# A kernel of attention, soft experts and a two-layer net: its rarely taken branch is put behind all products of the first expert layer

## The chip, the cores and the metric

The kernel runs on one core of one Trainium2 chip. The time is that of one execution on the device, in microseconds (us). Three runs of the kernel before the change gave 556.49, 556.83 and 557.16, median 556.83.

The engines: TensorE (PE, with its weight loads as PEld), VectorE (DVE), ScalarE (ACT), GpSimd (POOL) and SyncE (SP), which issues nearly all DMA transfers here. They run side by side and wait for one another by semaphores, which are counters.

## The reference

Three stages in a row, in float32:

```
attn:   scores = q k^T / 8 + bias(head, distance); keys kept: the first n_global
        and the last n_local up to the query; softmax; times v
        (4 batches, 8 heads, 768 positions, 64 wide; n_global = 8, n_local = 96)
x       = attn as 3072 tokens x 512
experts: logits = x @ phi                        # 32 slots, 4 for each of 8 experts
        d = softmax of logits over the tokens;  slot_in = d^T @ x
        slot_out[e] = relu(slot_in[e] @ w1[e]) @ w2[e]     # 512 x 1024, 1024 x 512
        c = softmax of logits over the slots;  x = c @ slot_out
net:    h = x @ w_in (512 x 2048);  g = relu(h)^2;  out = g @ w_out (2048 x 512)
```

## The kernel before, in words

The kernel runs in three stretches. Up to about 200 us it computes the attention in 48 units and routes each finished chunk of tokens to the slots; from about 254 us on it runs the two-layer net in five parts of unequal width (`WIDTHS`), each over 12 blocks of 256 tokens. The change lies between them, in the expert stage.

**Order.** The schedule is written out by hand: each engine runs its instructions in the order of the code. SyncE issues loads in that order too, and a load whose target is still being read holds back all loads behind it.

**Weights and places.** The expert weights w1_0 to w1_7 and w2_0 to w2_7 (2 MB each) and the raw 64-bit words of the net's first part (`win_0`, `wout_0`, 1 MB each) come in the order of `items`. `SLOTS` gives each a place: p0 to p7 hold w1; s0 to s2 hold w2_0 to w2_2; then p0, p1, p4, p5 take w2_3 to w2_6, p2 win_0, p7 w2_7 and p3 wout_0. A place is free when the products with what it held are done. `more()` issues the next load; w2_7 goes in four parts. `load_part(1)` brings the words of the second part into p0 and p1.

**The expert stage on TensorE.** `w1_of(e)` (L605 to L610) multiplies the slots' inputs by w1_e, 16 instructions in the trace, into two banks `pre0`, `pre1`. `hidden` (L671) evicts these (DVE and ACT), multiplies by a selecting matrix `si` (L678), runs seven warm-up products that compute nothing (`warm`), and takes the relu into `hZ` (L680). `w2_of(e)` (L684 to L690) multiplies by w2_e, 16 instructions in the trace, into `pSO`. Then come the sum's transposes and the first product of the net.

**Combine weights.** `combine` (L590) computes the softmax over the slots for all tokens. `copies(k)` (L649, DVE) repeats the result of six token tiles four times; `spread(k)` (L653) transposes them on TensorE (L658), ACT writes them into `cst` (L660) and DVE subtracts the rounded part (L661). There are four such groups, k = 0 to 3; they stand behind `w2_of(2)` to `w2_of(5)`.

**The branch.** The masks of the attention hold only for small n_local and n_global. A flag decides at L628 whether `general`, a slow path for any values (the dense path), computes everything again. With these inputs it is not taken. Five of the eight `w1_of` and `combine` stand ahead of it. The dense path uses the places of w2_3 and w2_4 for its own data, multiplies by w1 again (loading each into w2_3's place), and loads w2_3 and w2_4 again at its end (L636, L637): 344 loads in all. The compiled program has a short piece of its own for the side that skips it: each engine raises its counter by what the dense path would have raised it, so that what follows waits for the same values on both sides. SyncE does this for the eight counters to which loads report in turn; each of these instructions first waits until all loads issued on its counter have landed.

The lines around the branch:

```
    for e in range(EARLY):
        w1_of(e, wt[f"w1_{e}"])
        if SLOTS[nxt] == f"p{e}":
            more()
    combine()
    with tc.If(cond != 0, label="dense"):
        ...
    for e in range(EARLY, E):
        w1_of(e, wt[f"w1_{e}"])
        while nxt < NI and SLOTS[nxt] in [f"p{i}" for i in range(e + 1)]:
            more()
```

Of the kernel before, what the change touches and what calls it, by code (L numbers as in the profile page):

```python
# [7 lines left out]
F32 = mybir.dt.float32  # L8
F32R = mybir.dt.float32r
# [8 lines left out]
DM, NS, E, F = 512, 32, 8, 1024  # L18
DFF = 2048
NT = B * S  # L20
P = 128
# [7 lines left out]
NPRE = 8  # L29
# [10 lines left out]
def attention_moe_ffn(ctx: ExitStack, tc, qk, vx, nl, ng, phi, w1, w2, w_in, w_out, consts, relw, out):  # L40
    nc = tc.nc
    V, G = nc.vector, nc.gpsimd
# [5 lines left out]
    def full(name, shape, dt=F32):  # L48
        return cp.tile(shape, dt, tag=name, name=name)

    con = full("con", [P, C_R2])
# [16 lines left out]
    post = tc.alloc_tile_pool(name="post", bufs=1, side="right")  # L68
# [7 lines left out]
    def warm(n, src, dst):  # L76
        z = src.bitcast(BF16)
        for _ in range(n):
            nc.tensor.matmul(dst[:, 0:TB], lhsT=z[:, 0:P], rhs=z[:, 0:TB], start=True, stop=True)

    idle = aps.tile([P, 512], F32, tag="m", name="idle", bufs=4)
# [95 lines left out]
    def words(src, q):  # L177
        f0 = starts[q]
        return src[f0 * DM : (f0 + WIDTHS[q]) * DM].bitcast(I32).rearrange("(p c) -> p c", p=P)
# [3 lines left out]
    first = [(f"{n}_0", words(w, 0), [P, 2 * 4 * WIDTHS[0]], I32) for n, w in (("win", w_in), ("wout", w_out))]  # L183
    items[-1:-1] = first[:1]
    items += first[1:]
    NI = len(items)
    wt = {}
    SLOTS = [f"p{i}" for i in range(NPRE)] + ["s0", "s1", "s2"] + [f"p{i}" for i in (0, 1, 4, 5, 2, 7, 3)]

    def slot(tag, shape, dt, name):  # L190
        return (pre if tag[0] == "p" else stream).tile(shape, dt, tag=tag, name=name)

    def load_w(i, part=0, parts=1):
        name, src, shape, dt = items[i]
        if part == 0:
            wt[name] = slot(SLOTS[i], shape, dt, name)
        n = shape[1] // parts
        ps = slice(part * n, part * n + n)
        nc.sync.dma_start(wt[name][:, ps], src[:, ps])
# [302 lines left out]
    for i in range(NU - 2):  # L502
# [35 lines left out]
        if 4 <= i < 4 + NPRE * PARTS:  # L538
            load_w((i - 4) // PARTS, (i - 4) % PARTS, PARTS)
# [10 lines left out]
    i = NU - 2  # L550
# [26 lines left out]
    nxt = NPRE  # L577
    for _ in range(3):
        load_w(nxt)
        nxt += 1  # L580
# [9 lines left out]
    def combine():  # L590
        n = NT // P
        wide = rm.unsqueeze(2).broadcast_to([P, n, NS])
        V.tensor_reduce(rm, c_tok, axis=AX.X, op=ALU.max)
        V.tensor_tensor(c_tok, c_tok, wide, op=ALU.subtract)
        nc.scalar.activation(c_tok, c_tok, AF.Exp)
        V.tensor_reduce(rm, c_tok, axis=AX.X, op=ALU.add)
        V.tensor_scalar(rm, rm, EPS, None, op0=ALU.add)
        V.reciprocal(rm, rm)
        V.tensor_tensor(c_tok, c_tok, wide, op=ALU.mult)
# [5 lines left out]
    def w1_of(e, a):  # L605
        for n in range(2):
            for kc in range(4):
                z = e * 4 * NS + kc * NS
                nc.tensor.matmul(pp[n][kc * NS : kc * NS + NS, :], lhsT=slotZ[:, z : z + NS], rhs=a[:, kc, n * 512 : n * 512 + 512],  # L609
                                 start=e == 0, stop=e == E - 1)  # L610

    def more():
        nonlocal nxt
        if nxt < NI:
            n = 4 if nxt == NI - 2 else 1
            for j in range(n):
                load_w(nxt, j, n)
            nxt += 1

    EARLY = 5  # L620
    for e in range(EARLY):
        w1_of(e, wt[f"w1_{e}"])
        if SLOTS[nxt] == f"p{e}":
            more()
    combine()


    with tc.If(cond != 0, label="dense"):  # L628
        ta, tb = wt["w2_3"], wt["w2_4"]
        general(tc, nc, banks, qk, vx, relw, con, n_f, ta, tb, post, chunk_x, chunk_sums, route_start, route, slope8, ident)  # L630
        a = ta.rearrange("p a c -> p (a c)").rearrange("p (a c) -> p a c", c=F)
        for e in range(EARLY):
            nc.sync.dma_start(a, w1[e])
            w1_of(e, a)
        combine()
        nc.sync.dma_start(ta, w2[3])  # L636
        nc.sync.dma_start(tb, w2[4])  # L637
# [3 lines left out]
    ex = ctx.enter_context(tc.tile_pool(name="ex", bufs=1, side="right"))  # L641
# [3 lines left out]
    crs = {}  # L645

    SP = 6

    def copies(k):  # L649
        cr = crs[k] = ex.tile([P, SP, 4, NS], F32, tag="e", name=f"cr{k}", bufs=2)  # L650
        V.tensor_copy(cr, c_tok[:, SP * k : SP * k + SP, :].unsqueeze(2).broadcast_to([P, SP, 4, NS]))

    def spread(k):  # L653
        cr = crs.pop(k)
        for h in range(2):
            pc = bps.tile([P, 512], F32, tag="post", name=f"pc{k}_{h}", bufs=2)
            for t in range(3):
                nc.tensor.transpose(pc[:, t * P : t * P + P], cr[:, 3 * h + t, :, :].rearrange("p a s -> p (a s)"), ident)  # L658
            tok = slice((SP * k + 3 * h) * P, (SP * k + 3 * h + 3) * P)
            nc.scalar.copy(cst[:, tok], pc[:, 0 : 3 * P])  # L660
            V.tensor_tensor(cst[2 * NS : P, tok], pc[2 * NS : P, 0 : 3 * P], cst[2 * NS : P, tok].bitcast(F32), op=ALU.subtract)  # L661
        if k + 2 < NT // (SP * P):
            copies(k + 2)

    bps = tc.alloc_tile_pool(name="bps", bufs=1, space=PSUM)
    pSO = bps.tile([P, 512], F32, tag="so", name="pSO")


    HS = 8 * NS + 4

    def hidden(hZ):  # L671
        ev = ex.tile([P, F], F32, tag="e", name="ev", bufs=2)
        V.tensor_copy(ev[:, 0:512], pp[0])
        nc.scalar.copy(ev[:, 512:F], pp[1])
        ph = bps.tile([P, 512], F32, tag="sel", name="sel")
        idle = bps.tile([P, 512], F32, tag="post", name="idle3", bufs=2)
        for fc in range(8):
            nc.tensor.matmul(ph[:, NS * fc : NS * fc + NS], lhsT=ev[:, fc * P : fc * P + P], rhs=si, start=True, stop=True)  # L678
        warm(7, con, idle)
        V.tensor_scalar(  # L680
            hZ[:, 0 : E * HS].rearrange("p (e r) -> p e r", r=HS)[:, :, 0 : 8 * NS].rearrange("p e (f s) -> p e f s", s=NS)[:, :, :, 0:4],
            ph[:, 0 : 8 * NS].rearrange("p (f e s) -> p e f s", e=E, s=4), 0.0, None, op0=ALU.max)

    def w2_of(e):  # L684
        c = wt[f"w2_{e}"]
        for fc in range(8):
            g = fc % 4
            z = e * 8 * NS + fc * NS
            nc.tensor.matmul(pSO[g * NS : g * NS + NS, :], lhsT=hZ[:, z : z + NS], rhs=c[:, fc, :],  # L689
                             start=e == 0 and fc < 4, stop=e == E - 1 and fc >= 4)  # L690
# [19 lines left out]
    def load_part(q):  # L710
        raw[q] = []
        for nm, src, tag in (("win", w_in, "p0"), ("wout", w_out, "p1")):
            t = slot(tag, [P, 8 * WIDTHS[q]], I32, f"{nm}_{q}")
            nc.sync.dma_start(t, words(src, q))
            raw[q].append(t)

    def conv_in(q):
        W = WIDTHS[q]
        if q:
            f = slot("p4", [P, 4, W], F32, f"winf{q}").rearrange("p a c -> p (a c)")  # L720
        else:
            f = hZ[:, E * HS : E * HS + 4 * W]
        wq[q] = {"f": f.rearrange("p (a c) -> p a c", c=W)}
        for c0 in range(0, 4 * W, 512):
            yield from convert(raw[q][0], c0, f[:, c0 : c0 + 512], f"i{q}")
            yield
# [95 lines left out]
                V.tensor_tensor(o[:, cs], pa[:, cs], o[:, cs], op=ALU.add)  # L822
                eng.dma_start(out[k * P : k * P + P, cs], o[:, cs])

    for e in range(EARLY, E):
        w1_of(e, wt[f"w1_{e}"])
        while nxt < NI and SLOTS[nxt] in [f"p{i}" for i in range(e + 1)]:
            more()
        if e == E - 2:
            hZ = slot("p6", [P, 4096], F32, "hZ")  # L830
            G.memset(hZ[:, 0 : E * HS], 0.0)
    hidden(hZ)
    copies(0)
    copies(1)
    raw[0] = [wt["win_0"], wt["wout_0"]]
    w2_of(0)
    cu = slot("s0", [P, 4096], F32R, "cu")
    cst = cu[:, 0:NT]
    for e in range(1, E):
        if e == E - 1:  # L840
            load_part(1)
        w2_of(e)
        if 2 <= e < 6:
            spread(e - 2)
        if e == 5:
            for _ in conv_in(0):
                pass
# [3 lines left out]
    idle = bps.tile([P, 512], F32, tag="post", name="idle4", bufs=2)  # L851
# [9 lines left out]
    idle = fps.tile([P, 512], F32, tag="acc", name="idle5", bufs=3)  # L861
# [9 lines left out]
    next(c1)  # L871
    next(c0)
    warm(13, con, idle)
    oacc = [slot(t, [P, 8, DM], F32, f"oacc{i}") for i, t in enumerate(("p3", "p5", "p7"))]
    steps = [(q, n) for q in range(len(WIDTHS)) for n in range(NBLK)]
    AHEAD = 2
    for k in range(AHEAD):
# [16 lines left out]
    for i, (q, n) in enumerate(steps):  # L894
# [3 lines left out]
        for m in range(TB // P):  # L898
            j = 2 * n + m
# [169 lines left out]
```

## Time and profile before

| | us |
|---|---|
| median of three runs | 556.83 |
| profiled execution | 557.27 |
| its span, first to last instruction | 555.3 |
| PE busy | 532.4 (96%) |
| DVE busy | 399.3 (72%) |
| ACT busy | 310.7 (56%) |
| POOL busy | 165.5 (30%) |
| DMA, mean over the span | 161 GB/s |

The profile is of one execution. A row of a view names the engine, the line of the kernel (L689), the operation and the tiles, as out<-in with buffer numbers left out: all tiles of expert weights are `w`. "xN" is a count, and brackets hold the idle time before a row and what ended it. A "q" behind an engine (SPq) means its instruction queue, which waits, branches and issues transfers. The ends of TensorE's products are modelled; the start of the next one is the better mark. The granted clock is a share of TensorE's full 2.4 GHz; 0.50 is 1.2 GHz.

### The profile page before, as it was taken

To read this page: it belongs to the slowest core of one execution; us is meant where nothing else is said; L and a number is where in the kernel's file an instruction comes from. 1 tells how busy PE (TensorE), PEld (TensorE's weight loads), DVE (VectorE), ACT (ScalarE), POOL (GpSimd) and SP (SyncE) were. 2 spreads that over 40 slices of the span, in tenths; PEclk is the share of its full clock that TensorE was granted. 3 is DMA by queue.
4 is the path that set the end of the run, shared out by engine and by line. 5 is a ranking of instruction groups with operands and counts; after the bars stand their busy time and mean duration, and the time that the engine had idled before them with its cause. 6 is when DMAs were issued, how large, how long until landed. Compare 5 with 4: busy or idle time off the path is not lost.

```text
span 555.3 us, 10260 instructions
## 1 busy us (share of the span) xinstructions
PE 532.4 (96%) x3676; PEld 396.3 (71%) x3676; DVE 399.3 (72%) x998; ACT 310.7 (56%) x815; POOL 165.5 (30%) x147
## 2 busy tenths in 40 slices
PE   7999999999999999997999999999999999999997
PEld 4776767676767743345778687878888878888885
DVE  4888878888888771369778798796956857645553
ACT  3877778887877610236666556555544444534441
POOL 0000000000000001004375457543764536544441
PEclk9999999999999989999999999999999999999999
DMA  7789999998863589790440404011030000002333
GB/s 254 216 289 307 323 294 312 309 335 298 291 191 88 206 305 416 281 408 2 151 152 0 152 1 152 0 62 52 2 113 2 1 1 0 1 1 100 125 117 113
DMA packets 25834, 89.22 MB, mean 161 GB/s; under 512 B 3120, under 2 KB 3760, under 8 KB 23600
## 3 DMA queue, kind: packets, MB, share of 16 engines
q1 hardware_dynamic: 25344, 88.37, 45.1%
q8 instruction: 30, 0.49, 0.4%
q14 instruction: 28, 0.23, 0.1%
q10 hardware_dynamic: 432, 0.13, 0.1%
HBM read 82.20 MB, written 6.29 MB: 159 GB/s over the span
## 4 chain that ended last, share of the span: by engine, by line
PE 44%; DVE 11%; DMA 2%; ACT 2%; issue 1%; SPq 0%; POOL 0%; DVEq 0%; ACTq 0%; POOLq 0%
PE acc L808 13%; PE acc L809 13%; PE acc L810 12%; PE h L790 3%; DMA w<-in_w 2%; DVE rg L795 2%; DVE cvyo L700 2%; DVE cvyi L700 1%; DVE oacc L816 1%; DVE cvyi L699 1%; PE pre L609 1%; DVE cvyo L703 1%; PE pSO L689 1%; PE pu L749 1%; DVE winf L703 1%
## 5 line engine op out<-in xcount | busy, mean ns | idle before, releaser
L798 POOL TENSOR_TENSOR g<-rg,g 128x512 fp32r<-128x512 f32 (+1 forms) x109 | 136.2, 1251 | 140.4 <-DVE rg L795 135.3
L808 PE MATMUL acc<-w,g 128*128 128x512 f32 x384 | 151.7, 395 | 1.1 <-ACT g L797 0.6
L810 PE MATMUL acc<-w,g 128*128 128x512 f32 x384 | 150.1, 391 | 2.4 <-POOL g L798 2.3
L809 PE MATMUL acc<-w,g 128*128 128x512 f32 x384 | 150.8, 393 | 0.4 <-DVE w L739 0.4
L794 ACT ACTIVATE rg<-h 128x512 f32<-128x512 f32 (+1 forms) x109 | 59.6, 547 | 119.9 <-PE h L790 113.7
L816 DVE TENSOR_TENSOR oacc<-acc,oacc 128x512 f32<-128x512 f32 x95 | 65.3, 687 | 61.0 <-PE acc L810 60.8
L251 ACT ACTIVATE sm<-sm,nm 128x256 f32<-128x256 f32 (+1 forms) x192 | 92.2, 484 | 7.1 <-DVE nm L238 4.0
L810 PEld LDWEIGHTS acc<-w,g 128*128 128x128 f32 x384 | 72.1, 188 | 19.9 <-POOL g L798 4.3
L808 PEld LDWEIGHTS acc<-w,g 128*128 128x128 f32 x384 | 72.1, 188 | 18.3 <-issue 3.2
L809 PEld LDWEIGHTS acc<-w,g 128*128 128x128 f32 x384 | 72.4, 188 | 11.9 <-DVE w L739 0.7
L795 DVE SCALAR_TENSOR_TENSOR rg<-h,rg 128x512 f32<-128x512 f32 (+1 forms) x109 | 67.7, 621 | 15.7 <-ACT rg L794 15.6
L232 DVE CUSTOM_DVE_ANT_0 sm<-s,mask 128x256 f32<-128x256 f32 (+1 forms) x192 | 68.9, 396 | 0.8 <-PE s L218 0.5
L797 ACT ACTIVATE g<-rg 128x512 fp32r<-128x512 f32 (+1 forms) x109 | 63.3, 581 | 3.5
L384 POOL COPY l<-c_tok 128x256 f32<-128x256 f32 x11 | 4.4, 400 | 169.4 <-DVE c_tok L337 155.6
L218 PE MATMUL s<-raw 64*128 64x256 f32 (+1 forms) x384 | 52.4, 390 | 2.4 <-DVE mx L232 2.3
L279 PE MATMUL o<-pT,v 128*64 128x128 f32 x704 | 49.5, 280 | 2.9 <-DVE pT L268 2.4
L262 PE MATMUL pt<-con,sm 128*128 128x128 f32 x352 | 50.1, 281 | 1.5 <-DVE xb L330 1.1
L279 PEld LDWEIGHTS o<-pT,v 128*64 128x64 f32 x704 | 37.4, 136 | 18.9 <-DVE pT L268 5.0
L262 PEld LDWEIGHTS pt<-con,sm 128*128 128x128 f32 x352 | 38.5, 142 | 12.8 <-issue 11.4
L790 PEld LDWEIGHTS h<-cu 128*128 128x128 f32 x192 | 35.8, 188 | 7.9 <-ACT w L738 0.4
L268 ACT COPY pT<-pt 128x512 f32<-128x512 f32 x48 | 28.0, 584 | 21.5 <-PE pt L262 20.9
L790 PE MATMUL h<-cu 128*128 128x256 f32 x192 | 39.8, 280 | 0.2 <-ACT w L738 0.2
(141 smaller groups left out, 572.6 us busy)
## 6 DMA issues: line engine op xcount, KB each, us to landing
raw<-in_qk SPq DMA_DIRECT2D x48, 384.0 KB, 4.4
w<-in_w SPq DMA_DIRECT2D x36, 512.0 KB, 5.4
w<-in_w SPq DMA_DIRECT2D x7, 2048.0 KB, 9.5
v<-in_vx SPq DMA_DIRECT2D x48, 256.0 KB, 4.3
out_x<-oacc SPq DMA_DIRECT2D x23, 256.0 KB, 2.0
win<-in_w_in SPq DMA_DIRECT2D x2, 2048.0 KB, 8.4
wout<-in_w_out SPq DMA_DIRECT2D x2, 2048.0 KB, 7.9
win<-in_w_in SPq DMA_DIRECT2D x2, 1536.0 KB, 12.1
```

Source lines behind the costliest of these rows:

```text
L232: V.tensor_tensor_reduce(out=sm[:, j, 0:n, :], in0=sc[hh][:, tt, 0:n, :], in1=m[:, 2:3, :] if n == 1 else m[:, 0:2, :], scale=1.0, scalar= ...
L251: nc.scalar.activation(sm[:, j, 0:n, :], sm[:, j, 0:n, :], AF.Exp, bias=nm[:, j : j + 1], scale=QK_SCALE, accum_out=chunk_sums(i // NPR)[: ...
L262: nc.tensor.transpose(pp[tt][:, hh, c, :], sm[:, 2 * tt + hh, c, :], ident)
L279: nc.tensor.matmul(o[hh * D : hh * D + D, tt, :], lhsT=v[:, tt + 2 * c, hh * D : hh * D + D], rhs=pT[:, 2 * tt + hh, c, :], start=c == 0, ...
L790: nc.tensor.matmul(ph[:, k, :], lhsT=U[:, c0 : c0 + P], rhs=cst[:, n * TB : n * TB + TB], start=True, stop=True)
L795: V.scalar_tensor_tensor(g, ph[:, k0:k1, :], 0.0, r, op0=ALU.max, op1=ALU.mult)
L797: nc.scalar.activation(g2[:, 0, js, :], r, AF.Square)
L798: G.tensor_tensor(g2[:, 1, js, :], g, g2[:, 0, js, :].bitcast(F32), op=ALU.subtract)
L808: nc.tensor.matmul(pa, lhsT=ghi[:, j, ms], rhs=whi[:, j, :], start=j == 0, stop=False)
L809: nc.tensor.matmul(pa, lhsT=ghi[:, j, ms], rhs=wlo[:, j, :], start=False, stop=False)
L810: nc.tensor.matmul(pa, lhsT=glo[:, j, ms], rhs=whi[:, j, :], start=False, stop=j == J - 1)
L816: V.tensor_tensor(o, pa, o, op=ALU.add)
```

## The change

- All eight `w1_of` run ahead of the branch; the loads into the places that they free, down to `wout_0`, are issued there too, and `hZ` is made and cleared there. In the dense path all eight w1 are loaded and multiplied again.
- `win_0` and `wout_0` share place p2, as halves of one tile `raw_0`; `cu` (with `cst`) moves from s0 to p3, and the accumulator `oacc0` from p3 to s0.
- `copies(0)` and `copies(1)` write into a part of `hZ` that is free then, and stand ahead of `hidden`. In `hidden`, `spread(0)` stands between the eviction and the selecting products; the seven warm-up products are gone. `spread(1)`, `copies(2)` and `copies(3)` follow `hidden`; `spread(2)` and `spread(3)` stand behind `w2_of(2)` and `w2_of(3)`.

```diff
--- before.py
+++ after.py
@@ -185,14 +185,19 @@
     items += first[1:]
     NI = len(items)
     wt = {}
-    SLOTS = [f"p{i}" for i in range(NPRE)] + ["s0", "s1", "s2"] + [f"p{i}" for i in (0, 1, 4, 5, 2, 7, 3)]
+    SLOTS = [f"p{i}" for i in range(NPRE)] + ["s0", "s1", "s2"] + [f"p{i}" for i in (0, 1, 4, 5, 2, 7, 2)]
 
     def slot(tag, shape, dt, name):
         return (pre if tag[0] == "p" else stream).tile(shape, dt, tag=tag, name=name)
 
     def load_w(i, part=0, parts=1):
         name, src, shape, dt = items[i]
-        if part == 0:
+        if name == first[0][0]:
+
+            t = slot(SLOTS[i], [P, 2, shape[1]], dt, "raw_0")
+            for j in range(2):
+                wt[first[j][0]] = t[:, j, :]
+        elif part == 0 and name != first[1][0]:
             wt[name] = slot(SLOTS[i], shape, dt, name)
         n = shape[1] // parts
         ps = slice(part * n, part * n + n)
@@ -617,11 +622,16 @@
                 load_w(nxt, j, n)
             nxt += 1
 
-    EARLY = 5
-    for e in range(EARLY):
+    HS = 8 * NS + 4
+    free = []
+    for e in range(E):
         w1_of(e, wt[f"w1_{e}"])
-        if SLOTS[nxt] == f"p{e}":
+        free.append(f"p{e}")
+        while nxt < NI and SLOTS[nxt] in free:
             more()
+        if e == E - 2:
+            hZ = slot("p6", [P, 4096], F32, "hZ")
+            G.memset(hZ[:, 0 : E * HS], 0.0)
     combine()
 
 
@@ -629,7 +639,7 @@
         ta, tb = wt["w2_3"], wt["w2_4"]
         general(tc, nc, banks, qk, vx, relw, con, n_f, ta, tb, post, chunk_x, chunk_sums, route_start, route, slope8, ident)
         a = ta.rearrange("p a c -> p (a c)").rearrange("p (a c) -> p a c", c=F)
-        for e in range(EARLY):
+        for e in range(E):
             nc.sync.dma_start(a, w1[e])
             w1_of(e, a)
         combine()
@@ -646,8 +656,16 @@
 
     SP = 6
 
+    cu = slot("p3", [P, 4096], F32R, "cu")
+    cst = cu[:, 0:NT]
+
     def copies(k):
-        cr = crs[k] = ex.tile([P, SP, 4, NS], F32, tag="e", name=f"cr{k}", bufs=2)
+        if k < 2:
+
+            n = SP * 4 * NS
+            cr = crs[k] = hZ[:, E * HS + k * n : E * HS + k * n + n].rearrange("p (t a s) -> p t a s", a=4, s=NS)
+        else:
+            cr = crs[k] = ex.tile([P, SP, 4, NS], F32, tag="e", name=f"cr{k}", bufs=2)
         V.tensor_copy(cr, c_tok[:, SP * k : SP * k + SP, :].unsqueeze(2).broadcast_to([P, SP, 4, NS]))
 
     def spread(k):
@@ -659,24 +677,19 @@
             tok = slice((SP * k + 3 * h) * P, (SP * k + 3 * h + 3) * P)
             nc.scalar.copy(cst[:, tok], pc[:, 0 : 3 * P])
             V.tensor_tensor(cst[2 * NS : P, tok], pc[2 * NS : P, 0 : 3 * P], cst[2 * NS : P, tok].bitcast(F32), op=ALU.subtract)
-        if k + 2 < NT // (SP * P):
-            copies(k + 2)
 
     bps = tc.alloc_tile_pool(name="bps", bufs=1, space=PSUM)
     pSO = bps.tile([P, 512], F32, tag="so", name="pSO")
 
-
-    HS = 8 * NS + 4
 
     def hidden(hZ):
         ev = ex.tile([P, F], F32, tag="e", name="ev", bufs=2)
         V.tensor_copy(ev[:, 0:512], pp[0])
         nc.scalar.copy(ev[:, 512:F], pp[1])
         ph = bps.tile([P, 512], F32, tag="sel", name="sel")
-        idle = bps.tile([P, 512], F32, tag="post", name="idle3", bufs=2)
+        spread(0)
         for fc in range(8):
             nc.tensor.matmul(ph[:, NS * fc : NS * fc + NS], lhsT=ev[:, fc * P : fc * P + P], rhs=si, start=True, stop=True)
-        warm(7, con, idle)
         V.tensor_scalar(
             hZ[:, 0 : E * HS].rearrange("p (e r) -> p e r", r=HS)[:, :, 0 : 8 * NS].rearrange("p e (f s) -> p e f s", s=NS)[:, :, :, 0:4],
             ph[:, 0 : 8 * NS].rearrange("p (f e s) -> p e f s", e=E, s=4), 0.0, None, op0=ALU.max)
@@ -822,26 +835,20 @@
                 V.tensor_tensor(o[:, cs], pa[:, cs], o[:, cs], op=ALU.add)
                 eng.dma_start(out[k * P : k * P + P, cs], o[:, cs])
 
-    for e in range(EARLY, E):
-        w1_of(e, wt[f"w1_{e}"])
-        while nxt < NI and SLOTS[nxt] in [f"p{i}" for i in range(e + 1)]:
-            more()
-        if e == E - 2:
-            hZ = slot("p6", [P, 4096], F32, "hZ")
-            G.memset(hZ[:, 0 : E * HS], 0.0)
-    hidden(hZ)
     copies(0)
     copies(1)
+    hidden(hZ)
+    spread(1)
+    copies(2)
+    copies(3)
     raw[0] = [wt["win_0"], wt["wout_0"]]
     w2_of(0)
-    cu = slot("s0", [P, 4096], F32R, "cu")
-    cst = cu[:, 0:NT]
     for e in range(1, E):
         if e == E - 1:
             load_part(1)
         w2_of(e)
-        if 2 <= e < 6:
-            spread(e - 2)
+        if 2 <= e < 4:
+            spread(e)
         if e == 5:
             for _ in conv_in(0):
                 pass
@@ -871,7 +878,7 @@
     next(c1)
     next(c0)
     warm(13, con, idle)
-    oacc = [slot(t, [P, 8, DM], F32, f"oacc{i}") for i, t in enumerate(("p3", "p5", "p7"))]
+    oacc = [slot(t, [P, 8, DM], F32, f"oacc{i}") for i, t in enumerate(("s0", "p5", "p7"))]
     steps = [(q, n) for q in range(len(WIDTHS)) for n in range(NBLK)]
     AHEAD = 2
     for k in range(AHEAD):
```

## Rows read from the trace of the kernel before

**Rows 1.** the chain of waits, 203 to 256 us: start, us, what.

```profile
221.69 3.62 PE pSO L689 x32
...
227.87 13.56 DMA w<-in_w
...
254.27 0.35 DVE cvyi L699
```

**Rows 2.** SyncE's waits, 200 to 250 us: total, times, longest.

```profile
SPq L628 <- SPq L628: 11.9, 3, 5.5
```

**Rows 3.** instructions of L628: ns min/median/max, first and last start.

```profile
L628 SPq EVENT_SEMAPHORE  x8: 17/17/17, 218.3 to 225.0; - x8
...
L628 SPq COMPARE_BRANCH  x1: 73/73/73, 212.7 to 212.7; - x1
```

**Rows 4.** SyncE in order of time: issues of w2_5, w2_6, wout_0.

```profile
212.31 0.33 SPq L199 DMA_DIRECT2D w<-in_w  x1
...
225.09 0.34 SPq L199 DMA_DIRECT2D w<-in_w  x1
...
228.38 0.50 SPq L199 DMA_DIRECT2D wout<-in_w_out  x1
```

**Rows 5.** these three loads: KB, us from issue to landing.

```profile
w<-in_w SPq DMA_DIRECT2D x1, 2048.0 KB, 12.3
...
w<-in_w SPq DMA_DIRECT2D x1, 2048.0 KB, 7.8
...
wout<-in_w_out SPq DMA_DIRECT2D x1, 1024.0 KB, 15.5
```

**Rows 6.** stretches: busy times; last, granted clock, DMA share, GB/s.

```profile
206.50:222.30 15.80, 14.43 (x135) 5.70 (x131) 4.31 (x9) 0.58 (x1) 1.83 (x1) 1.00 0.96 391
222.30:226.10 3.80, 3.80 (x40) 1.17 (x36) 0.09 (x1) 0.00 (x0) 0.00 (x0) 1.00 0.13 41
...
228.00:242.00 14.00, 13.29 (x98) 4.00 (x90) 8.80 (x16) 4.23 (x9) 0.00 (x0) 1.00 1.00 416
...
194.10:197.40 3.30, 3.30 (x15) 1.24 (x14) 2.44 (x4) 0.00 (x0) 0.00 (x0) 0.50 0.95 407
250.30:252.30 2.00, 0.02 (x1) 0.02 (x1) 1.46 (x3) 0.87 (x3) 0.72 (x1) 1.00 0.01 6
```

**Rows 7.** TensorE in order of time: start, us, what, count.

```profile
203.46 8.79 PE L609 MATMUL pre<-w,slotZ 128*32 128x512 f32 x80 [0.45 <-DVE slotZ L460]
...
213.58 5.36 PE L609 MATMUL pre<-w,slotZ 128*32 128x512 f32 x48 [1.33 <-DVEq L628]
...
221.62 5.36 PE L689 MATMUL pSO<-w,hZ 128*32 128x512 f32 x48
226.91 0.87 PE L658 MATMUL pc<-con,cr 128*128 128x128 f32 x6
227.71 1.92 PE L689 MATMUL pSO<-w,hZ 128*32 128x512 f32 x16
...
230.37 1.92 PE L689 MATMUL pSO<-w,hZ 128*32 128x512 f32 x16
...
241.48 1.05 PE L689 MATMUL pSO<-w,hZ 128*32 128x512 f32 x4 [0.20 <-DMA w<-in_w]
242.46 0.72 PE L79 MATMUL idle<-con 128*128 128x256 bf16 x5
```

**Rows 8.** warm-up products in order of time, at start and later.

```profile
1.46 5.37 PE L79 MATMUL idle<-zero 128*128 128x256 bf16 x26 [1.46 <-DVE zero L74]
...
246.39 1.58 PE L79 MATMUL idle<-con 128*128 128x256 bf16 x13
```

**Rows 9.** POOL and DVE in order of time, 217 to 222 us.

```profile
217.31 1.83 POOL L831 MEMSET hZ<- 128x2080 f32 x1 [27.83 <-DMA w<-in_w]
...
221.37 1.02 DVE L651 COPY cr<-c_tok 128x768 f32<-128x768 f32 x2
```

## The prediction

> **What bounds the kernel now.** I read the chain of waits first, in the stretch that the diff touches. TensorE multiplies there by the second-layer expert weights (`w2_of`, L689), and the chain shows that its end is set by a load: the last quarter of w2_7 is issued at 227.87 and on its way for 13.56 us [rows 1]. So the question is why that load is late. SyncE's waits answer it: 11.9 us at L628, the branch, in three waits, the longest 5.5 [rows 2]. The branch's own line shows what it does there: it decodes the branch at 212.7 and then runs eight semaphore instructions, the first at 218.3 and the last at 225.0 [rows 3]. Between them lies the load issued at 212.31 (w2_5); the next load, w2_6, is issued at 225.09 [rows 4]. w2_5 lands 12.3 us after its issue, at 224.6 [rows 5]: SyncE goes on when it has landed. The DMA engines have run dry meanwhile (0.13 of their time and 41 GB/s from 222.3 to 226.1, against 1.00 and 416 GB/s later) [rows 6].
>
> The program's listing says why. On the side that skips the dense path, each engine adds to its counter what the dense path would have added, so that later waits hold on both sides. For the loads this is SyncE's job: eight counters, and for each one instruction that waits until every load issued so far on that counter has landed, and only then adds 688 (43 dense loads of 16). The dense path overwrites the tiles of w2_3 and w2_4. So the first product with w2_3 (expert 3) waits for two of these counters at a value that needs the addition, and the first with w2_4 for five more. Now that costs nothing: the additions are done at 225.0, and the products of w2_3 begin at 227.71 [rows 7].
>
> **What the change does to this: the hold.** It is the largest term, so it comes first. The loads of w2_6, win_0, w2_7 in four parts and wout_0 move ahead of the branch on SyncE. They no longer wait for w2_5's landing (w2_6 goes out at about 213.8, w2_7 at about 217.3), but the eight additions now wait for all of them. They stand in order of the counters. By the round of eight in which the loads take them, the first addition waits for w2_7's last part, the second for wout_0, the very last load. The dense path then has 347 loads (three more w1 loads), and its reload of w2_3 reports to the fourth counter. So the products of w2_3 can't start before wout_0 has landed, though they don't read it, nor can those of w2_4.
>
> When does it land? Behind w2_5, which lands at 224.6, stand 2048 + 1024 + 4 x 512 + 1024 KB = 6.29 MB. At the 416 GB/s of the second stretch [rows 6] that is 15.1 us: 239.7. By the landings of before: w2_6 at 225.09 + 7.8 = 232.9, wout_0 at 228.38 + 15.5 = 243.9 [rows 4, 5], 11.0 us apart; with 5.0 us for w2_6 itself behind w2_5 this gives 240.6. I take the middle, 240.2. Two more additions, 0.07 us each as in the run of the last ones in rows 3, and the signal's way make it 240.4.
>
> On the rate a rule of the Trainium skill differs. Its page "DMA: Bandwidth & Descriptors", section "Where 436 GB/s comes from", puts the limit of loads from HBM near 358 GB/s for a core; by it the 6.29 MB would take 17.6 us, and the end would be 2 us later (an estimate from that page; rival 3). The trace does not agree, with 416 GB/s over 14 us, and decides.
>
> **The products behind the hold.** From 240.4 TensorE has still to do: w2_3 and the transposes of `spread(3)`, 2.66 us (227.71 to 230.37 for such a pair); w2_4 to w2_7, 64 products at the pace of 48 in 5.29 us (221.62 to 226.91, where the next transposes begin), 7.05 us; and the tail from the last products to the next instruction, 0.98 us less 0.44 for four products, 0.54 [rows 7]. End: 250.65, where it is 242.46 now. That is +8.2 us at full clock.
>
> **The clock.** TensorE will have stood idle for some 12 us: w2_0 to w2_2 and `spread(2)` are done at about 228.5 (below). Before has no idle stretch of this length with products behind it except the start: there 26 warm-up products take 5.37 us, 0.207 us each, and 13 of the same kind later take 1.58, 0.122 each [rows 8]. At that pace the 26 would have taken 2.2 us less. After a mild pause the clock was granted at 0.50, 1.2 GHz, from 194.1 to 197.4 [rows 6]; 3.4 us at half pace lose 1.7. At the other end stands a pause of 2 us at 250.3 with the clock at full level throughout: nothing lost [rows 6]. An idle time of 12 us is nearest to the start; I take 2.0 us, and 0 to 2.2 as the ends. Sum: +10.2 us.
>
> **The other edits, all under that cover.** Up to the hold TensorE has time to spare, so these decide nothing, but their place has to be checked.
> - All 128 products of w1 run without a break: 8.79 and 5.36 us less one tail of 0.5 from 203.46, to 217.1 instead of 218.9; the gap of 1.33 us at the branch [rows 7] moves behind them. A gain of 0 to 1.8 us, used up by the hold.
> - POOL clears hZ before its branch: 1.83 us [rows 9] from about 215.5. DVE's first instruction behind the branch waits for POOL and TensorE to have passed theirs, about 217.4. Its two copies (1.02 us together [rows 9]) now stand ahead of the eviction that the selecting products need. Up to 1.3 us later; were an engine to come to the far side of the branch as late as SyncE does, 5.6 us after the decoding [rows 3], up to 5.6.
> - `spread(0)` and `spread(1)`, 0.87 us of transposes each [rows 7], move ahead of w2_0; seven warm-up products go. w2_0 then begins at about 222.3 instead of 221.62, at worst 227. It has to be done with w2_2 by 240.4 and takes 6.2 us with `spread(2)`: a cover of 12 us, or 7 at worst.
> - `conv_in(0)` on DVE follows `spread(3)`, so now behind the hold: some 4 us of work from about 246.5, done before the copy of the result at about 254. If that cover were short, under 1 us.
> - win_1 is issued when w2_3's products are done, about 244.5. It finds the queue empty: 1.57 MB, 3.8 us, and the 2.8 us that w2_6 took beyond its own 5.0, landing at 251. Its first use, now at 254.27 [rows 1], is 10 us later too. Hidden.
> - `cu`, `oacc0` and the raw words change places: no instruction more, and every tile they take over has been read long before. Nothing, from -0.1 to 0.1.
>
> From the end of w2_7 on, the same chain follows as now (DVE and ACT convert, then the main loop), all of it behind these products, so the shift reaches the end unshortened.
>
> **Sum.** The profiled execution: 555.3 us of span and 2.0 around it, 557.27. With +10.2 it is 567.5. The median of the runs shown is 0.44 lower: 567.0. Ends: landing at 239.7 and no clock lost, +7.7, 564.5; landing at 240.6 and 2.2 lost, +10.6, 567.4. A slower burst of loads adds to that (rival 3).
>
> **Rivals.**
> 1. Faster: the hold doesn't exist, because the products of w2_3 and w2_4 wait for their own loads only. Then the loads of w2_6 and w2_7, no longer stopped at the branch, end early: w2_7's last part 2.5 us (1 MB) ahead of wout_0, at 237.7; its four products and tail 0.98, 238.7. TensorE itself would be there: 222.3 + 15.9 of products and transposes = 238.2. That is 3.7 us before 242.46: 553.1. For it: the idle DMA engines of rows 6 and the chain through the last load. Against it: the waits in the listing, and rows 3, where SyncE's additions stand and last until a landing. The Trainium skill speaks for it: "DMA: Bandwidth & Descriptors", "Rules for kernel authors", advises to issue a DMA early, compute, and wait for it late; the trace agrees as far as the load's issue goes, the wait is what this case moves the wrong way.
> 2. A shorter hold: w2_3 waits for one of the first counters only and starts 2.5 us earlier, w2_4 is held until 240.4. The end is 2.7 us earlier than forecast: 564.3.
> 3. A longer hold: eight loads at once run slower. At the 391 GB/s of 206.5 to 222.3, where the engines also ran dry for a moment, they would take 16.1 us and land at 240.7, within the ends; for 2 us more, 569.0, they would have to keep to 368, and no busy row in rows 6 is so slow. The limit that the Trainium skill's page states, above, would give this case.
> 4. No change: no hold, but w2_7's last part lands as late as now, since the branch was not what delayed it. Against it stand rows 4 and 5, w2_5's landing and w2_6's issue 0.5 us apart: 556.8.
>
> **Chances.** Forecast 0.74, rival 2 0.09, rival 1 0.08, rival 3 0.06, rival 4 0.03. The forecast's own range is 564.5 to 567.4; with rivals 2 and 3 and their spread the range for 8 in 10 is 563.5 to 569. Under 0.2% (1.1 us), about what a measurement of this kernel can tell, counts as no change. Faster 0.08, same 0.03, slower 0.89.
>
> **What would show it.** The hold: SyncE's semaphore instructions at L628 last until about 240, the DMA engines are busy without a gap from 206 to about 238, and TensorE is idle from about 228.5 until 240.4, between w2_2 and w2_3. The clock: a row at half level around 240 to 245. The cover: w2_0 begins near 222. The forecast is wrong if w2_3's products start before 235, or if wout_0 lands well off 240.

## The result and the profile after

The changed kernel takes 565.39 us (median of four runs, 564.73 to 566.12), the kernel before 557.00 beside it: a ratio of 1.0148, interval 1.0128 to 1.0169. The change costs 8.4 us. The forecast was 567.0, +10.2.

The branch now stands at L638, the second expert products at L702. First the branch's line and SyncE's waits, which answer to rows 2 and 3.

```profile
L638 SPq EVENT_SEMAPHORE  x8: 17/17/17, 236.1 to 239.0; - x8
...
L638 POOLq COMPARE_BRANCH  x1: 59/59/59, 214.9 to 214.9; - x1
...
L638 POOLq EVENT_SEMAPHORE  x1: 17/17/17, 216.8 to 216.8; - x1
L638 SPq COMPARE_BRANCH  x1: 73/73/73, 219.8 to 219.8; - x1
```

```profile
SPq L638 <- SPq L638: 18.6, 2, 16.2
```

SyncE decodes the branch at 219.8 and runs its eight additions from 236.1 to 239.0, with 18.6 us of waiting, where it was 11.9. The landings of w2_5 (issued at 211.48) and of wout_0 (issued at 219.32), KB and us to landing, answer to [rows 5]:

```profile
w<-in_w SPq DMA_DIRECT2D x1, 2048.0 KB, 12.2
...
raw<-in_w_out SPq DMA_DIRECT2D x1, 1024.0 KB, 19.2
```

w2_5 lands at 223.7, wout_0 at 238.5. TensorE in order of time, to be read beside [rows 7]:

```profile
202.62 13.94 PE L614 MATMUL pre<-w,slotZ 128*32 128x512 f32 x128 [0.45 <-DVE slotZ L465]
217.83 0.85 PE L676 MATMUL pc<-con,hZ 128*128 128x128 f32 x6 [1.26 <-DVE hZ L669]
...
221.46 5.36 PE L702 MATMUL pSO<-w,hZ 128*32 128x512 f32 x48
226.75 0.87 PE L676 MATMUL pc<-con,cr 128*128 128x128 f32 x6
238.85 3.52 PE L702 MATMUL pSO<-w,hZ 128*32 128x512 f32 x16 [11.23 <-SPq L638]
242.30 0.87 PE L676 MATMUL pc<-con,cr 128*128 128x128 f32 x6
243.11 7.07 PE L702 MATMUL pSO<-w,hZ 128*32 128x512 f32 x64
250.11 0.94 PE L79 MATMUL idle<-con 128*128 128x256 bf16 x7
```

After w2_2 and the transposes at 226.75 TensorE stands still for 11.23 us, and the profile names SyncE's branch line as what it waited for. w2_3 starts at 238.85, 0.35 us behind wout_0's landing. Its 16 instructions, 1.92 us before, take 3.52. From the first w1 product to the first instruction behind w2_7 it is 250.11 - 202.62 = 47.49 us; before, 242.46 - 203.46 = 39.00. That is 8.49 us, all of the loss: from that mark to the end of the span it is 312.9 us, and it was 312.8. (The stage begins 0.84 us earlier here; such starts differ by up to 1.9 us from profile to profile, so times are counted from the first w1 product below.)

The stretches (busy times; then granted clock, DMA share, GB/s):

```profile
222.30:236.10 13.80, 5.32 (x50) 1.81 (x42) 2.55 (x6) 0.86 (x2) 0.00 (x0) 0.85 0.99 408
231.90:242.10 10.20, 3.25 (x16) 0.68 (x16) 0.00 (x0) 0.00 (x0) 0.00 (x0) 0.50 0.46 188
243.20:250.10 6.90, 6.90 (x64) 1.88 (x64) 4.59 (x8) 1.74 (x4) 0.00 (x0) 1.00 0.94 366
262.70:266.00 3.30, 3.30 (x9) 2.52 (x9) 3.30 (x5) 2.04 (x4) 1.41 (x2) 0.50 0.00 0
```

In the first the DMA engines are busy throughout, where they had run dry [rows 6]; so the change does what its load order promises. In the second the clock is at 0.50, 1.2 GHz: 231.9 to 242.1, that is 3.3 us into the products. It is full for the other expert products, and at half once more for 3.4 us from 262.7, early in the net, which lengthens nothing: there DVE sets the pace.

### The profile page after: what moved, and what is told of

Its sections match the earlier page's. It is cut to its first block, busy times and chain, and to the rows that moved or that the text cites. A ratio compares the mean times of both kernels' runs of the same rounds, so it can differ in the third digit from the quotient of the medians.

```text
span 563.0 us, 10247 instructions
## 1 busy us (share of the span) xinstructions
PE 529.9 (94%) x3669; PEld 397.1 (71%) x3669; DVE 399.3 (71%) x998; ACT 310.8 (55%) x815; POOL 165.6 (29%) x147
## 3 DMA queue, kind: packets, MB, share of 16 engines
HBM read 82.20 MB, written 6.29 MB: 157 GB/s over the span
## 4 chain that ended last, share of the span: by engine, by line
PE 43%; DVE 11%; ACT 1%; issue 1%; POOL 0%; DVEq 0%; ACTq 0%; POOLq 0%
PE acc L821 13%; PE acc L822 12%; PE acc L823 12%; PE h L803 3%; DVE rg L808 2%; PE pSO L702 2%; DVE cvyo L713 2%; DVE oacc L829 1%; DVE cvyi L713 1%; DVE cvyi L712 1%; DVE cvyo L716 1%; DVE cvyo L712 1%; DVE winf L716 1%; DVE oacc L827 1%; ACT rg L807 1%
## 5 line engine op out<-in xcount | busy, mean ns | idle before, releaser
L808 DVE SCALAR_TENSOR_TENSOR rg<-h,rg 128x512 f32<-128x512 f32 (+1 forms) x109 | 67.7, 621 | 15.6 <-ACT rg L807 15.6
L284 PEld LDWEIGHTS o<-pT,v 128*64 128x64 f32 x704 | 37.4, 136 | 18.7 <-DVE pT L273 5.1
```

The source lines that it names most:

```text
L284: nc.tensor.matmul(o[hh * D : hh * D + D, tt, :], lhsT=v[:, tt + 2 * c, hh * D : hh * D + D], rhs=pT[:, 2 * tt + hh, c, :], start=c == 0, ...
L808: V.scalar_tensor_tensor(g, ph[:, k0:k1, :], 0.0, r, op0=ALU.max, op1=ALU.mult)
```

## The experiments

Theory: the hold. w2_3 and w2_4 wait for SyncE's additions, and these for every load issued ahead of the branch. Rivals: the moved copies and transposes (or the shared place) cost the time; or the branch itself holds the engines, whatever the loads do. Each kernel's stage is counted from its own first w1 product ("stage": to the first instruction behind w2_7). Each ratio is to the kernel before as it ran beside that kernel, with medians from 557.0 to 557.3:

| kernel | median us | ratio, interval | w2_3 starts, us into the stage | stage us | from there to the end of the span |
|---|---|---|---|---|---|
| before | 557.0 | | 24.3 | 39.0 | 312.8 |
| after | 565.39 | 1.0148 [1.0128, 1.0169] | 36.2 | 47.5 | 312.9 |
| a_pool | 559.45 | 1.0050 [1.0032, 1.0068] | 32.6 | 42.2 | 313.3 |
| a_pool2 | 554.6 | 0.9955 [0.9938, 0.9972] | 24.9 | 35.9 | 313.5 |
| b_pool | 554.1 | 0.9950 [0.9933, 0.9966] | 23.9 | 35.7 | 312.9 |
| a_wout | 564.08 | 1.0121 [1.0103, 1.0139] | 34.1 | 45.9 | 312.9 |
| a_warm | 564.29 | 1.0136 [1.0116, 1.0156] | 36.2 | 45.9 | 313.0 |
| a_late | 560.4 | 1.0051 [1.0032, 1.0070] | 24.9 (w2_6: 37.4) | 43.7 | 312.7 |
| b_move | 568.29 | 1.0202 [1.0182, 1.0222] | 37.4 | 51.3 | 312.6 |

**a_pool: no additions on SyncE.** In `general` and in the body of the branch:

```diff
-            nc.sync.dma_start(a, w1[e])
+            nc.gpsimd.dma_start(a, w1[e])
...
```

> The changed kernel, with the loads inside the dense path issued by POOL instead of SyncE: they then report to other counters, and SyncE has nothing to add when the path is skipped. Theory (the hold: w2_3 waits for SyncE's additions, which wait for wout_0): TensorE goes on from w2_2 to w2_3 without a pause, the products of w2_7 end some 12.3 us earlier (at 237.8 instead of 250.1), the kernel takes about 553. Rival (the moved copies and transposes, or the shared place, cost the time): no change, about 565.

Measured 559.45: the theory's hold is gone, but the number is missed by 6 us. TensorE in order of time, then POOL's instructions at the branch, then DVE's first one behind it:

```profile
203.42 13.94 PE L614 MATMUL pre<-w,slotZ 128*32 128x512 f32 x128 [0.45 <-DVE slotZ L465]
222.28 1.52 PE L676 MATMUL pc<-con,hZ 128*128 128x128 f32 x6 [4.92 <-DVE hZ L669]
...
235.97 1.92 PE L702 MATMUL pSO<-w,hZ 128*32 128x512 f32 x16
...
245.63 0.94 PE L79 MATMUL idle<-con 128*128 128x256 bf16 x7
```

```profile
L638 POOLq EVENT_SEMAPHORE  x5: 17/43/43, 221.3 to 221.7; - x5
...
L638 POOLq COMPARE_BRANCH  x1: 59/59/59, 215.7 to 215.7; - x1
```

```profile
221.38 0.23 DVE L654 CAST si4r<-con 128x128 fp32r<-128x128 f32 x1 [12.69 <-POOLq L638]
```

SyncE has no semaphore instruction left at the branch, and no pause stands before w2_3 any more. A new one stands ahead of the first transposes, 4.92 us: DVE makes their input and waits 12.69 us for POOL's branch line. POOL decodes its branch at 215.7 and is on the far side at 221.3, 5.6 us later; in the changed kernel it took 214.9 to 216.8 (first fence of the section on the result). With all dense loads in it, the piece that POOL skips has become long. TensorE then ran at half clock from 221.3 to 231.5 by the profile's clock records, so the selecting products took 3.46 us instead of 1.94.

**a_pool2: the same, and POOL branches early.** The clearing of hZ, which kept POOL ahead of its branch until 217, goes back behind it:

```diff
-            G.memset(hZ[:, 0 : E * HS], 0.0)      # in the loop over w1
+    G.memset(hZ[:, 0 : E * HS], 0.0)              # behind the branch
```

> The changed kernel with the dense loads issued by POOL, and the clearing of hZ moved back behind the branch. In a_pool DVE waited until 221.4 for POOL, which reached the far side of its branch 5.6 us after decoding it, and TensorE fell to half clock; now POOL decodes the branch before 190, as in b_pool. Theory (the hold was all, and a_pool's remainder was POOL): no pause at the branch beyond 1.3 us, none before w2_3, the products of w2_7 end 34.5 us after the first w1 product, as their last load lands, against 39.0 in the kernel before: 552.6. Rival (something else in the moved copies costs too): 555 or more.

```profile
202.99 13.94 PE L614 MATMUL pre<-w,slotZ 128*32 128x512 f32 x128 [0.45 <-DVE slotZ L465]
...
227.91 1.92 PE L702 MATMUL pSO<-w,hZ 128*32 128x512 f32 x16
...
237.90 1.05 PE L702 MATMUL pSO<-w,hZ 128*32 128x512 f32 x4 [0.23 <-DMA w<-in_w]
238.88 0.94 PE L79 MATMUL idle<-con 128*128 128x256 bf16 x7
```

Measured 554.6. Both pauses are gone, and the end is set by w2_7's last part, 0.23 us of waiting. The stage is 35.9 us long instead of 34.5, since that part lands later than counted (at 237.9, 34.9 us into the stage, after 33.5 in the changed kernel). What delays it is not shown. The loads of the second part, which start at 229.94 here, do not explain it: w2_6, which lands 0.3 us behind their start, is already 1.3 us later than in the changed kernel (27.3 us into the stage, after 26.0), and in b_move, where they start at 243.78, w2_7's last part lands 34.6 us into the stage as well. 2.7 us less than before, 10.8 less than the change alone: the moved copies, transposes and places cost nothing that shows.

**b_pool: the kernel before, without SyncE's additions.**

> The kernel before, with the same edit: dense loads by POOL. Theory: SyncE passes its branch at about 218.3 without waiting for w2_5's landing, w2_6 goes out some 6.5 us earlier, the DMA engines don't run dry, and TensorE no longer waits for w2_7's parts: -2.8 us, about 554. Rival (the branch itself, its code, holds SyncE until 225): no change, 557.

```profile
202.89 8.79 PE L609 MATMUL pre<-w,slotZ 128*32 128x512 f32 x80 [0.45 <-DVE slotZ L460]
212.68 5.36 PE L609 MATMUL pre<-w,slotZ 128*32 128x512 f32 x48 [1.00 <-DVEq L628]
...
234.79 3.82 PE L689 MATMUL pSO<-w,hZ 128*32 128x512 f32 x32
238.55 0.94 PE L79 MATMUL idle<-con 128*128 128x256 bf16 x7
```

```profile
222.30:226.10 3.80, 3.80 (x37) 1.00 (x30) 0.00 (x0) 0.00 (x0) 0.00 (x0) 1.00 1.00 418
```

Measured 554.1, as the theory had it. The DMA engines move 418 GB/s from 222.3 to 226.1, where they had moved 41 [rows 6], and the last 32 products run without a wait for a load. So the additions cost the kernel before some 3 us already. (The edit also shortens the piece that SyncE skips: w2_6 goes out at 214.67, 2.5 us after the decoding at 212.1, where the first addition had stood 5.6 us behind it. These rows do not price the two apart.) It is as fast as a_pool2: the intervals of the two overlap almost wholly.

**a_wout: one load fewer ahead of the branch.** wout_0 is issued behind it.

```diff
-        while nxt < NI and SLOTS[nxt] in free:
+        while nxt < NI - 1 and SLOTS[nxt] in free:
...
+    more()
     post.release()
```

> The changed kernel, with the one load of wout_0 (1 MB) issued behind the branch. Theory: the additions then wait for w2_7's last part only, which lands 2.4 us earlier; w2_3 starts at about 236.4 instead of 238.85: -2.4 us, about 563. Rival (w2_3 is held by something else, such as its own load or DVE): no change.

```profile
204.35 13.94 PE L614 MATMUL pre<-w,slotZ 128*32 128x512 f32 x128 [0.45 <-DVE slotZ L465]
...
238.42 3.64 PE L703 MATMUL pSO<-w,hZ 128*32 128x512 f32 x16 [7.46 <-SPq L638]
241.99 1.28 PE L677 MATMUL pc<-con,cr 128*128 128x128 f32 x6
...
250.20 0.94 PE L79 MATMUL idle<-con 128*128 128x256 bf16 x7
```

```profile
L638 SPq EVENT_SEMAPHORE  x8: 17/17/17, 238.1 to 238.6; - x8
```

w2_3 starts 34.1 us into the stage instead of 36.2: 2.1 of the 2.4 us. The stage is shorter by 1.6, the kernel by 1.3. The rest of the stage's gain went to the clock: its half level, from 236.1 to 242.9, reached here into the transposes behind w2_3, which took 1.2 us to the next product instead of 0.8, and w2_3 itself took 0.1 longer. (It was at half from 222.4 to 225.8 too, but what this slowed stands ahead of the hold and is covered by it.) The hold moves with the last load ahead of the branch, which w2_3 doesn't read.

**a_warm: the hold filled.** 96 warm-up products between `spread(2)` and w2_3.

```diff
+NWARM = 96
...
+        if e == 2:
+            warm(NWARM, con, bps.tile([P, 512], F32, tag="sel", name="idle3"))
```

> The changed kernel, with 96 warm-up products that compute nothing on TensorE between the transposes of spread(2) and w2_3: they fill the hold. Theory: the hold stays, the half clock goes; w2_3's 16 products take 1.9 us instead of 3.5: -1.7 us, about 563.7. Rival (the idle clock is the larger part of the loss): down to 557.

```profile
227.28 10.64 PE L80 MATMUL idle<-con 128*128 128x256 bf16 x96
238.66 1.92 PE L703 MATMUL pSO<-w,hZ 128*32 128x512 f32 x16 [0.73 <-SPq L639]
...
248.33 0.94 PE L80 MATMUL idle<-con 128*128 128x256 bf16 x7
```

The hold ends as before, 36.2 us into the stage, and w2_3 takes 1.92 us instead of 3.52. The stage is shorter by 1.6 us, which is the price of the clock. The medians differ by 1.1, and their intervals overlap; the rows carry this reading.

**a_late: other tiles shared.** The dense path works in the tiles of w2_6 and w2_7.

```diff
-        ta, tb = wt["w2_3"], wt["w2_4"]
+        ta, tb = wt["w2_6"], wt["w2_7"]
...
-        nc.sync.dma_start(ta, w2[3])
-        nc.sync.dma_start(tb, w2[4])
+        nc.sync.dma_start(ta, w2[6])
+        nc.sync.dma_start(tb, w2[7])
```

> The changed kernel, with the tiles of w2_6 and w2_7 as the dense path's scratch instead of those of w2_3 and w2_4. SyncE's additions stay and end as late as before (36.2 us after the first w1 product). Theory: w2_3 to w2_5 run without a pause, only w2_6 is held; two expert products instead of five and a spread stand behind the hold: -7.2 us at full clock, -5.5 if part of them runs at half: 558 to 560. Rival (TensorE is held as a whole by the branch, whichever tiles are shared): no change, 565.

```profile
230.12 3.64 PE L702 MATMUL pSO<-w,hZ 128*32 128x512 f32 x32
239.97 6.29 PE L702 MATMUL pSO<-w,hZ 128*32 128x512 f32 x32 [6.21 <-SPq L638]
246.20 0.94 PE L79 MATMUL idle<-con 128*128 128x256 bf16 x7
```

w2_3 to w2_5 run through, and the pause (6.21 us) stands where the shared tiles are first read. Measured 560.4, 0.4 above the forecast's upper end: in this profile wout_0 landed 1.2 us later than in the changed kernel, and the clock was at half until 245.4, so the 32 products behind the hold took 6.2 us; in b_pool the last 32, at full clock, took 3.8. Its ten runs spread from 557.47 to 562.29; what sets this spread was not tried.

**b_move: the branch alone moved.** The kernel before with all eight w1 products, the loads and the clearing ahead of the branch, and nothing else of the change.

> The kernel before, with the branch behind all eight w1 products and nothing else of the change (copies, transposes, warm-ups and places as before). Theory: the same hold, and two more groups of transposes behind it (0.87 us each): 1.7 us over the changed kernel, 567. Rival (the moved copies and transposes are the loss): 557.

```profile
240.04 3.64 PE L693 MATMUL pSO<-w,hZ 128*32 128x512 f32 x16 [13.35 <-SPq L634]
243.61 1.54 PE L664 MATMUL pc<-con,cr 128*128 128x128 f32 x6
...
253.98 0.94 PE L79 MATMUL idle<-con 128*128 128x256 bf16 x7
```

568.29: the branch's place alone makes the loss, and the rest of the change gives back 2.9 us of it, more than the 1.7 for the transposes. In this profile the hold lasted 1.2 us longer, since the loads landed later, and the half clock reached into the transposes (1.54 us for 0.87).

## Why the prediction was right, step by step

- **The hold** was the step on which all rests, and it holds: it goes when SyncE has nothing to add (a_pool2, b_pool), moves with the last load (a_wout), follows the shared tiles (a_late), and comes with the branch's place alone (b_move). The eight additions also waited as forecast: two waits, the first until 236.1, the second 2.4 us, until wout_0's landing at 238.5.
- **The landing** of wout_0 was put 15.6 us behind w2_5's, and was 14.8: 6.29 MB at 425 GB/s. Of the two ends (15.1 and 16.0) the steady rate, 416 GB/s, was the nearer one; the landings of before, issued up to 228.38, shared the DMA engines with the word loads of the second part, issued at 229.74 and 232.95. The 358 GB/s of the Trainium skill ("DMA: Bandwidth & Descriptors", "Where 436 GB/s comes from") was again not what the trace shows: 425 GB/s.
- **The products behind it** were put at 10.25 us and took 11.26 - 1.6 = 9.66. The failing term is the tail: 0.54 was taken from the last four products, where the next instruction stands 0.98 us behind their start; behind 64 products in a row the whole is 7.00 us (243.11 to 250.11 above), where 7.05 and 0.54 were added up.
- **The clock** was put at 2.0 us and cost 1.6, by the 16 products of w2_3 and by a_warm. The row from 194 (1.7) was nearer than the start of the kernel (2.2), from which the value was raised.
- Together the shift of the stage was forecast 1.7 us too high: 0.8 in the landing, 0.6 in the products, 0.4 in the clock, less 0.1 for the way from the landing to w2_3, put at 0.2 us and 0.35 long. All three large terms were put too high, so nothing cancelled. The upper end of the forecast's own range leaves this 0.2 out, which the lower end has in it: 567.6 by its own terms, not 567.4.
- **The cover** was right: w2_0 began 18.84 us into the stage, where 222.3 - 203.46 = 18.84 was forecast ("about 222.3", so the last digits are luck), and nothing on DVE, ACT or POOL came late. Of rival 1, the time without a hold, a_pool2 shows what it was worth: 554.6, where 553.1 was worked out.

## What to carry to other kernels

A branch that is never taken still has a price: in this program the side that skips it brings the counters up to date, and for loads this means waiting until everything in flight has landed. So look for what is in flight where the branch stands, not only for what it interrupts, and for who first reads a tile that the branch could have written. Where the skipped path reports its loads to counters that the main path doesn't use, as in b_pool, the wait is gone; but the engine that then issues them takes longer past its branch, so it has to branch early (a_pool and a_pool2).

## What was not expected of the hardware

How long an engine needs to the far side of a branch changes here with the loads that stand in the path it skips. POOL took 1.9 us after the change (214.9 to 216.8) and 5.6 in a_pool, with all dense loads in its path; where it branches early, 1.2 us before (188.3 to 189.5) and 5.7 in a_pool2 (189.3 to 195.0). SyncE took 5.6 us to its first addition before [rows 3] with these loads in its path; without them its first instruction behind the branch stood 1.3 us behind the decoding in a_pool (220.5 to 221.8) and 0.2 in a_pool2 (220.1 to 220.3). The Trainium skill, "Runtime: NRT & Kernel Launch", "Instruction fetch mechanics", says that a taken branch to code outside the two blocks that an engine holds must first fetch it; the rows of POOL and SyncE fit this and give a price that the page leaves open, but no run shows that the time is this fetch. The amount of skipped code alone does not order the engines: in the profile after, DVE took 5.8 us (206.9 to 212.7), ACT 3.3 (204.5 to 207.8) and TensorE 2.8 (213.8 to 216.6), though `general` has more instructions for TensorE than for DVE (by its code 14 against 8 for each head of a token tile). In a_pool POOL's 5.6 us turned a side remark of the forecast, up to 5.6 us at the branch and covered by the hold, into 4.92 us of pause, after 1.26 in the changed kernel, once the cover was gone.
